# First mixture of an attention and two-mixture kernel: one pass over all 16 inner tiles, weights earlier, attention spread over more steps

## The chip, the cores and the metric

The kernel runs on one core of one Trainium2 chip. A core has five engines that run side by side, each through its own instructions in a fixed order: TensorE (PE, matrix products), VectorE (DVE), ScalarE (ACT), GpSimd (POOL) and SyncE (SP), which here issues nearly all DMAs. PE writes its products to PSUM, which DVE and ACT empty. The metric is the device time of one execution in microseconds (us); lower is better. The kernel before takes 1975.65 us (median of three runs, 1974.85 to 1976.97).

## The reference, cut to what matters

```python
# attention: batch 4, 8 heads, 576 positions, head size 64; float32
scores = q @ k.T / sqrt(64);  mask: a window of 32 positions for heads 0 to 3,
                              every 4th of 128 positions for heads 4 to 7
x = softmax(scores) @ v       # -> 2304 tokens x 512
# first mixture ("rational"): w_in 512 x 2048, w_out 2048 x 512, both float64
h = x @ w_in
P = a[0] + a[1]*h + a[2]*h*h + a[3]*h*h*h
Q = 1 + abs(b[0])*abs(h) + abs(b[1])*h*h
x2 = (P / (Q + 1e-6)) @ w_out
# second mixture: 8 experts, w1 512 x 1024 and w2 1024 x 512 each, float32
G = exp(x2 @ w_gate - max), then 8 rounds of normalising rows and columns
out = sum over e of G[:, e] * (relu(x2 @ w1[e]) @ w2[e])
```

The float64 weights reach the chip as pairs of 32-bit words; the kernel builds float32 values from them with integer operations.

## The kernel before, in words

The 2304 tokens are six blocks (n = 0 to 5) of 384; the 2048 inner columns are 16 tiles f of 128. One step of the first mixture is one (block, tile) pair: `rat_l1` (12 float16 matmuls, since each operand is split into a high and a low half) makes h in a PSUM bank, `rat_a`, `rat_q`, `rat_b` and `rat_c` form the rational function on DVE, ACT and POOL, and `rat_l2` (12 matmuls) adds the step's product with w_out to four PSUM banks `ob` that belong to the block. There are 96 steps. PE works on `rat_l1` of step g and `rat_l2` of step g - 5 (`LAG`).

`SEQ` (L620) is the order of the steps. The kernel before runs blocks 0 to 3 in two passes (L619): steps 0 to 31 take tiles 0 to 7 of blocks 0, 1, 2, 3, steps 32 to 63 take tiles 8 to 15 of the same blocks, and steps 64 to 95 all 16 tiles of blocks 4 and 5. At the end of a block's pass `x2_evac` (L710) empties the four banks: after the first pass by ACT copies (L717) into x2's place in SBUF, after the second by DVE additions to what lies there (L715).

The program falls into these stages. In the first, which I call the prelude, the attention of batch 0 runs, and the first quarters of w_in are loaded and converted. Then come the 96 steps with the attention of batches 1 to 3 strewn in by `ATT` (L1137): batch 1 over steps 0 to 7, batch 2 over 7 to 23, batch 3 over 40 to 62. A batch gives one and a half blocks. An attention batch is 52 pieces: 16 `prep` (transposes of q and k on PE, copies by ACT), 12 `qk`, 12 `tr` and 12 `av`. The second mixture follows, with its L1 products (L921) and L2 products (L1021 to L1023) on PE; its expert weights are prepared by DVE, ACT and POOL, those of expert 0 during steps 65 to 95 (`raw_absmax`, `raw_diff`, `raw_split`, L845 to L890).

Each step has four slots; `at(s, ...)` hangs work on slot s and `run_slot` runs it. So are hung: the conversion of w_in's quarters c = 1 to 3 (`wi_conv`, `wi_scale`, `wi_split`, from step `WI_S[c]` on, L1139), that of w_out's 16 tiles (`wo_split(f)` at step `WO[f]`, L1138, its load four slots ahead), the maximum over a finished block (`x2_absmax`, L721) and the mixing of two blocks for the second mixture (`mix_sub`, `mix_put`, L738, L742). Conversion of one 128x512 tile is `to_f32` (L489): one ACT copy (L492) and three DVE operations: a shift (L496), a shift with an or for the low bits (L497), an and with an or for the sign (L498). A w_in tile then has a pass for its maximum on ACT (L527) and a split by ACT and DVE (L229, L232); a w_out tile has a copy on ACT (L609) and a subtraction on POOL (L613).

Loads go out on SP's queue in order. `load` (L165) ties a load to the newest matmul that opens a step, so that loads are paced by PE. SBUF is laid out by hand (`HOME`): rooms R2 and R3 hold first q and k of attention pairs that are loaded ahead (`LOADS`, L1158) and later quarters 2 and 3 of w_in; room W3 holds a second pair of transposed q and k for batches 0 and 1 (`alt`, L336) and later the raw quarter 3.

The order in which each engine runs its instructions is not that of the program alone: a planner takes the instructions in program order as priority, attention pieces with a bonus, simulates when each is ready, and lets a later one pass an earlier one that is not ready. `pin` (L824) forbids this for one instruction: it must follow the one last noted in `behind`. Before, `pin` is used for weight preparation of the second mixture alone, and `behind` is empty during the 96 steps.

Of the kernel before, what the change touches and what calls it, by code (L numbers as in the profile page):

```python
# [22 lines left out]
SIGN = -(1 << 31)  # L23
# [5 lines left out]
def kernel(  # L29
# [20 lines left out]
    P = 128  # L50
# [180 lines left out]
    def split_lo(src, hi, lo, s):  # L231
        nc.vector.scalar_tensor_tensor(out=lo, in0=src, scalar=s, in1=hi, op0=ALU.mult, op1=ALU.subtract)  # L232
# [98 lines left out]
    def att_prep(b, pr, x):  # L331
# [4 lines left out]
        alt = b < 2 and pr % 2  # L336
# [152 lines left out]
    def to_f32(src, y, dst):  # L489
        w = src.rearrange("p (n two) -> p n two", two=2)  # L490
        lo, hi = w[:, :, 0], w[:, :, 1]
        nc.scalar.activation(y, hi.bitcast(F32), AF.Copy, scale=float(2.0**-112))  # L492
        d = y.bitcast(I32)

        def bits():
            nc.vector.tensor_scalar(out=d, in0=d, scalar1=3, scalar2=None, op0=ALU.logical_shift_left)  # L496
            nc.vector.scalar_tensor_tensor(out=d, in0=lo, scalar=29, in1=d, op0=ALU.logical_shift_right, op1=ALU.bitwise_or)  # L497
            nc.vector.scalar_tensor_tensor(out=dst.bitcast(I32), in0=hi, scalar=SIGN, in1=d, op0=ALU.bitwise_and, op1=ALU.bitwise_or)  # L498

# [44 lines left out]
    def wo_load(f):  # L544
        t = xhome(5 if f in (1, 3, 5) else 3)
# [26 lines left out]
    def wi_scale(c):  # L572
        return pow2_scale(wmx[:, 4 * c:4 * c + 4], 4, 14, s_wi[:, c:c + 1], i_wi[:, c:c + 1], lag=3 if c > 1 else 0, then=lambda: coefs(0, c, c + 1))
# [10 lines left out]
    def wg_prep():  # L584
        m = cols()
        nc.vector.tensor_reduce(out=m, in_=wgr.rearrange("p k e -> p (k e)"), axis=AX, op=ALU.max, apply_absolute_value=True)
        pow2_scale(m, 1, 4, s_wg, i_wg)
        split16(wgr, wg[:, :, 0:NE], wg[:, :, NE:], s_wg)()
# [28 lines left out]

    cur = {}
    PASSES = [(n, f0, f0 + 8) for f0 in (0, 8) for n in range(4)] + [(n, 0, NF1) for n in range(4, NB)]  # L619
    SEQ = [(n, f, f == f0, f == f1 - 1) for n, f0, f1 in PASSES for f in range(f0, f1)]  # L620
# [24 lines left out]
    def pair(st, x):  # L645
        if st // 2 % 2 == 0:
            return room(f"I{x}0", [P, 2, TB], F32)
        return room(f"I{x}1" + ("b" if 54 <= st < 78 else "a"), [P, 2, TB], F32)

    def rat_a(st):  # L650
# [6 lines left out]
        nc.vector.scalar_tensor_tensor(out=t, in0=t, scalar=a1, in1=hp, op0=ALU.add, op1=ALU.mult)  # L657
# [7 lines left out]
    def rat_b(st):  # L665
# [5 lines left out]
        nc.vector.scalar_tensor_tensor(out=g, in0=g, scalar=na0, in1=r, op0=ALU.add, op1=ALU.mult)  # L671
# [10 lines left out]
    def rat_l2(st, half):  # L682
# [11 lines left out]
        if half == 1:  # L694
            cur.pop(st)
            if last:
                x2_evac(n, f == NF1 - 1)
# [4 lines left out]
    x2p = {}  # L702
# [7 lines left out]
    def x2_evac(n, final):  # L710
        t = xhome(n).rearrange("p (k t) -> p k t", k=KD)
        part = x2p.pop(n, None)
        for dd in range(KD):
            if part is not None:
                nc.vector.tensor_tensor(out=t[:, dd, :], in0=ob[dd], in1=part[:, dd, :], op=ALU.add)  # L715
            else:
                nc.scalar.activation(t[:, dd, :], ob[dd], AF.Copy)  # L717
# [703 lines left out]
```

## Time and profile before

| | us |
|---|---|
| median of three runs (lowest, highest) | 1975.65 (1974.85, 1976.97) |
| the profiled execution's own time | 1978.19 |
| its span, first to last instruction | 1976.1 |
| busy: POOL | 491.1 |
| busy: PE's weight loads (PEld), beside the matmuls | 1418.3 |

The page of the profile gives busy times of each engine and, in 40 slices of about 49 us, the busy tenths and the TensorE clock that was granted, in tenths of full speed. A busy engine can be one that runs at half clock. The views that follow are windows (busy time of each engine between two moments), waits (who waited for whom), timelines (instructions in order) and groups of instructions by line. Line numbers are those of the kernel before. The windows below cut the span where PE starts the first L1 matmul of step 0 (68.93 us), of step 15 (207.31), of step 39 (318.62) and of step 60 (442.98), and where the last L2 matmul of step 95 ends (631.45). In a row of a window the busy times stand in the order PE, PEld, DVE, ACT, POOL; where a tile or a line is asked for, engines without such instructions are left out of it.

### The profile page before, as it was taken

How to read it: one execution, taken by the hardware profiler on the slowest of the kernel's cores; microseconds unless marked ns; L12 is line 12 of the kernel's file. 1: busy time of each engine (PE TensorE's matmuls, PEld its weight loads, DVE VectorE, ACT ScalarE, POOL GpSimd, SP SyncE). 2: the span in 40 equal slices, each digit the busy share in tenths (PEclk: the TensorE clock that was granted, in tenths of full speed). 3: DMA queues.
4: the chain of work that ended last, by engine and by line, in shares of the span. 5: the costliest groups of instructions: out<-in, count | busy, mean ns of one | idle time of the engine just before them, and what ended most of it. 6: DMA issues, size and time to landing. Idle time of an engine off the chain costs nothing. (4 is left out here: it accounts for less than half of the span.)

```text
span 1976.1 us, 36600 instructions
## 1 busy us (share of the span) xinstructions
PE 1886.4 (95%) x14202; PEld 1418.3 (72%) x14202; DVE 1567.5 (79%) x2564; ACT 1217.0 (62%) x2182; POOL 491.1 (25%) x489
## 2 busy tenths in 40 slices
PE   6688999998999999999999999999999999999998
PEld 5466777776767677767777777777777777777776
DVE  5797788799997998778787777877877787786754
ACT  5777777775776645646565664655555565555542
POOL 1232334321222113014212311411421141141111
PEclk7789999999999999999999999999999999999999
DMA  6643221124310451565356346345435625543323
GB/s 181 165 140 87 50 68 34 34 67 144 109 44 17 150 163 59 175 171 155 68 136 154 69 110 174 68 103 142 111 62 131 166 65 117 159 91 79 83 56 53
DMA packets 213133, 207.92 MB, mean 105 GB/s; under 512 B 78432, under 2 KB 160864, under 8 KB 212960
## 3 DMA queue, kind: packets, MB, share of 16 engines
q1 hardware_dynamic: 196096, 173.09, 29.1%
q0 software_dynamic: 16864, 32.51, 11.0%
q8 instruction: 111, 1.82, 0.4%
q14 instruction: 62, 0.51, 0.1%
HBM read 155.86 MB, written 49.68 MB: 104 GB/s over the span
## 5 line engine op out<-in xcount | busy, mean ns | idle before, releaser
L921 PEld LDWEIGHTS <-roomA 128*128 128x128 f16 x3276 | 319.7, 98 | 181.5 <-issue 14.6
L921 PE MATMUL l1a<-roomA 128*128 128x384 f16 x1872 | 357.0, 326 | 5.3 <-ACT roomV L970 4.2
L921 PE MATMUL l1b<-roomA 128*128 128x384 f16 x1404 | 273.6, 326 | 4.0 <-DVE roomA L972 1.9
L943 POOL TENSOR_TENSOR roomIG<-roomA 128x384 f32<-128x384 f32 x48 | 59.7, 1244 | 455.6 <-ACT roomA L977 354.6
L1021 PE MATMUL yps<-roomA 128*128 128x256 f16 x630 | 169.7, 273 | 2.2 <-DVE roomV L1047 1.5
L1022 PE MATMUL yps<-roomA 128*128 128x256 f16 x630 | 170.7, 273 | 0.8 <-DVE roomA L884 0.8
L1022 PE MATMUL yps<-roomA,roomV 128*128 128x256 f16 x630 | 170.5, 273 | 0.1
L677 POOL TENSOR_TENSOR roomIG<-roomA,roomIG 128x384 fp32r<-128x384 f32 x96 | 116.6, 1225 | 213.6 <-ACT roomIG L676 184.1
L1023 PE MATMUL yps<-roomA,roomV 128*128 128x256 f16 x630 | 169.6, 273 | 0.0
L1023 PE MATMUL yps<-roomA 128*128 128x256 f16 x630 | 168.9, 273 | 0.0
L1021 PE MATMUL yps<-roomA,roomV 128*128 128x256 f16 x630 | 168.8, 273 | 0.1
L692 PE MATMUL o1ps<-roomIG,roomV 128*128 128x384 f32 x384 | 136.2, 355 | 4.0 <-POOL roomIG L677 3.8
L870 POOL TENSOR_TENSOR roomA<-roomA 128x256 f32<-128x256 f32 x140 | 130.7, 953 | 35.2 <-DVE roomA L884 23.3
L631 PE MATMUL h1ps<-roomA 128*128 128x384 f16 x384 | 130.5, 340 | 8.8 <-ACT p L390 4.2
L884 DVE SCALAR_TENSOR_TENSOR roomA<-roomA,sm 128x768 f16<-128x768 f32 (+1 forms) x92 | 114.5, 1257 | 24.7 <-ACT roomA L881 23.9
L693 PE MATMUL o1ps<-roomIG,roomV 128*128 128x384 f32 x384 | 130.6, 340 | 0.0
L632 PE MATMUL h1ps<-roomA 128*128 128x384 f16 x384 | 130.1, 339 | 0.3 <-DVE roomA L232 0.3
L633 PE MATMUL h1ps<-roomA 128*128 128x384 f16 x384 | 129.8, 338 | 0.0
L943 POOL TENSOR_TENSOR roomIG<-roomV 128x384 f32<-128x384 f32 x48 | 50.1, 1044 | 299.5 <-ACT roomV L977 248.7
L691 PE MATMUL o1ps<-roomIG,roomV 128*128 128x384 f32 x384 | 107.5, 363 | 15.9 <-ACT roomIG L676 15.8
L1021 PEld LDWEIGHTS <-roomA 128*128 128x128 f16 x1008 | 98.7, 98 | 28.5 <-DVE roomA L1047 3.4
L881 ACT ACTIVATE roomA<-roomA,sm 128x768 f16<-128x768 f32 (+1 forms) x92 | 93.7, 1035 | 37.4 <-POOL roomA L870 17.8
(224 smaller groups left out, 4958.3 us busy)
## 6 DMA issues: line engine op xcount, KB each, us to landing
roomA<-xd SPq DMA_DIRECT2D x119, 384.0 KB
roomA<-in_moe_w_dram SPq DMA_DIRECT2D x256, 128.0 KB
roomA<-in_moe_w_dram SPq DMA_DIRECT2D x128, 256.0 KB
out_dram<-roomV POOLq DMA_DIRECT2D x31, 512.0 KB, 5.8
out_dram<-roomA POOLq DMA_DIRECT2D x31, 512.0 KB, 5.8
roomV<-in_moe_w_in_dram SPq DMA_DIRECT2D x16, 512.0 KB
roomA<-in_moe_w_out_dram SPq DMA_DIRECT2D x16, 512.0 KB
xd<-roomA SPq DMA_DIRECT2D x14, 384.0 KB
```

Source lines behind the costliest of these rows:

```text
L631: mm = nc.tensor.matmul(hp, whi, xb[:, 0, kk, :], start=kk == 0, stop=False)
L632: nc.tensor.matmul(hp, whi, xb[:, 1, kk, :], start=False, stop=False)
L633: nc.tensor.matmul(hp, wlo, xb[:, 0, kk, :], start=False, stop=kk == KD - 1)
L677: nc.gpsimd.tensor_tensor(out=gl, in0=g, in1=gh.bitcast(F32), op=ALU.subtract)
L692: nc.tensor.matmul(ob[dd], hi, d["gl"], start=False, stop=False)
L693: nc.tensor.matmul(ob[dd], lo, d["gh"], start=False, stop=last)
L870: pin("p" if pool else "v", eng.tensor_tensor(out=d[:, o, :], in0=a, in1=b, op=ALU.add if w == 0 and n == 0 else ALU.subtract))
L884: pin("v", nc.vector.scalar_tensor_tensor(out=l, in0=x, scalar=sc, in1=h, op0=ALU.mult, op1=ALU.subtract))
L921: mm = nc.tensor.matmul(ps, w[:, wx_, wh, kk * P:(kk + 1) * P], x[:, xh, kk, :], start=start and kk == 0 and wh == 0 and xh == 0, stop=sto ...
L1021: nc.tensor.matmul(o, hh[:, a - 1, c], w[:, m, 0, :], start=i == 0 and half == 0, stop=False)
L1022: nc.tensor.matmul(o, hh[:, a - 1, c], w[:, m, 1, :], start=False, stop=False)
L1023: nc.tensor.matmul(o, hl[:, a - 1, c], w[:, m, 0, :], start=False, stop=i == NP - 1 and (last or half == 1 or b == 3))
```

## The change

- The first mixture runs each block through all 16 tiles at once: steps 16n to 16n + 15 belong to block n. No partial sums remain; `x2_evac` is four ACT copies per block.
- So quarters 2 and 3 of w_in and tiles 8 to 15 of w_out are due at steps 8, 12 and, for w_out, 8 + 5 to 15 + 5. `WI_S` goes from (0, 8, 14) to (0, 4, 7.5), `WO` of tiles 8 to 15 from 20 to 34 to 11.75 to 16.75, the loads of the two quarters from 16 and 14 slots to 6 and 4 slots ahead of their step, and the lag in `wi_scale` from 3 slots to 1. w_out tiles are staged in two places in turn for all f.
- Attention: batch 1 over steps 0 to 14, batch 2 over 15 to 38, batch 3 over 39 to 62. R2, R3 and W3 are no longer free for batch 1, so its q and k are loaded one pair ahead only, and its transposed q and k have one place.
- `to_f32`: the ACT copy becomes a parametric relu with slope -2^32 for negative values, whose result keeps the sign in the right bit; the third DVE operation (L498) goes.
- The gate weights are loaded at step 20 and prepared at step 26 instead of in the prelude.
- x2 work (`x2_absmax`, `mix_sub`, the low half in `mix_put`) is tied by `pin` behind the newest of the rational function's DVE operations (L657 or L671, noted in `behind`). Since `behind` now holds an entry during the steps, the expert-0 preparations that used `pin` all along are tied too.

```diff
-SIGN = -(1 << 31)
...
     def split_lo(src, hi, lo, s):
-        nc.vector.scalar_tensor_tensor(out=lo, in0=src, scalar=s, in1=hi, op0=ALU.mult, op1=ALU.subtract)
+        return nc.vector.scalar_tensor_tensor(out=lo, in0=src, scalar=s, in1=hi, op0=ALU.mult, op1=ALU.subtract)
...
-        alt = b < 2 and pr % 2
+        alt = b < 1 and pr % 2
...
-        nc.scalar.activation(y, hi.bitcast(F32), AF.Copy, scale=float(2.0**-112))
+        nc.scalar.activation(y, hi.bitcast(F32), AF.Prelu, scale=float(2.0**-112), alpha=-float(2.0**32))
...
-            nc.vector.scalar_tensor_tensor(out=d, in0=lo, scalar=29, in1=d, op0=ALU.logical_shift_right, op1=ALU.bitwise_or)
-            nc.vector.scalar_tensor_tensor(out=dst.bitcast(I32), in0=hi, scalar=SIGN, in1=d, op0=ALU.bitwise_and, op1=ALU.bitwise_or)
+            nc.vector.scalar_tensor_tensor(out=dst.bitcast(I32), in0=lo, scalar=29, in1=d, op0=ALU.logical_shift_right, op1=ALU.bitwise_or)
...
-        t = xhome(5 if f in (1, 3, 5) else 3)
+        t = xhome(5 if f % 2 else 3)
...
-        return pow2_scale(wmx[:, 4 * c:4 * c + 4], 4, 14, s_wi[:, c:c + 1], i_wi[:, c:c + 1], lag=3 if c > 1 else 0, then=lambda: coefs(0, c, c + 1))
+        return pow2_scale(wmx[:, 4 * c:4 * c + 4], 4, 14, s_wi[:, c:c + 1], i_wi[:, c:c + 1], lag=1 if c > 1 else 0, then=lambda: coefs(0, c, c + 1))
...
-        pow2_scale(m, 1, 4, s_wg, i_wg)
-        split16(wgr, wg[:, :, 0:NE], wg[:, :, NE:], s_wg)()
+        return pow2_scale(m, 1, 4, s_wg, i_wg, lag=3, then=lambda: split16(wgr, wg[:, :, 0:NE], wg[:, :, NE:], s_wg)())
...
-    PASSES = [(n, f0, f0 + 8) for f0 in (0, 8) for n in range(4)] + [(n, 0, NF1) for n in range(4, NB)]
-    SEQ = [(n, f, f == f0, f == f1 - 1) for n, f0, f1 in PASSES for f in range(f0, f1)]
+    SEQ = [(n, f, f == 0, f == NF1 - 1) for n in range(NB) for f in range(NF1)]
...
-        return room(f"I{x}1" + ("b" if 54 <= st < 78 else "a"), [P, 2, TB], F32)
+        return room(f"I{x}1" + ("b" if 58 <= st < 78 else "a"), [P, 2, TB], F32)
...
-        nc.vector.scalar_tensor_tensor(out=t, in0=t, scalar=a1, in1=hp, op0=ALU.add, op1=ALU.mult)
+        behind["v"] = nc.vector.scalar_tensor_tensor(out=t, in0=t, scalar=a1, in1=hp, op0=ALU.add, op1=ALU.mult).ins.name
...
-        nc.vector.scalar_tensor_tensor(out=g, in0=g, scalar=na0, in1=r, op0=ALU.add, op1=ALU.mult)
+        behind["v"] = nc.vector.scalar_tensor_tensor(out=g, in0=g, scalar=na0, in1=r, op0=ALU.add, op1=ALU.mult).ins.name
...
-    def x2_evac(n, final):
+    def x2_evac(n):
         t = xhome(n).rearrange("p (k t) -> p k t", k=KD)
-        part = x2p.pop(n, None)
         for dd in range(KD):
-            if part is not None:
-                nc.vector.tensor_tensor(out=t[:, dd, :], in0=ob[dd], in1=part[:, dd, :], op=ALU.add)
-            else:
-                nc.scalar.activation(t[:, dd, :], ob[dd], AF.Copy)
-        if not final:
-            x2p[n] = t
+            nc.scalar.activation(t[:, dd, :], ob[dd], AF.Copy)
...
-        nc.vector.tensor_reduce(out=xmx[:, n:n + 1], in_=xhome(n), axis=AX, op=ALU.max, apply_absolute_value=True)
+        pin("v", nc.vector.tensor_reduce(out=xmx[:, n:n + 1], in_=xhome(n), axis=AX, op=ALU.max, apply_absolute_value=True))
...
-        nc.vector.tensor_tensor(out=mix_src(G, c), in0=mix_src(G, a), in1=mix_src(G, b), op=ALU.subtract)
+        pin("v", nc.vector.tensor_tensor(out=mix_src(G, c), in0=mix_src(G, a), in1=mix_src(G, b), op=ALU.subtract))
...
-            split_lo(src, t[:, 0, :], t[:, 1, :], s)
+            pin("v", split_lo(src, t[:, 0, :], t[:, 1, :], s))
...
-    ATT = ((1, 0, 7), (2, 7, 23), (3, 40, 62))
-    WO = [f + f // 7 if f < 8 else 20 + 2 * (f - 8) for f in range(NF1)]
-    WI_S = (None, 0, 8, 14)
+    ATT = ((1, 0, 14), (2, 15, 38), (3, 39, 62))
+    WO = [f if f < 8 else 11.75 + (f - 8) // 2 * 1.5 + 0.5 * (f % 2) for f in range(NF1)]
+    WI_S = (None, 0, 4, 7.5)
...
-    LOADS = {a: (c,) for a, c in zip(allp, allp[1:]) if a >= (1, 3)}
-    LOADS.update({(0, 2): ((1, 1, "R2"),), (0, 3): ((1, 0), (1, 3, "R3")), (1, 0): ((1, 2),), (1, 2): ((2, 0),)})
-    LOADS.pop((1, 3))
+    LOADS = {a: (c,) for a, c in zip(allp, allp[1:]) if a >= (0, 3)}
...
-            at(s + (14 if c > 1 else 11) + kk, wi_split, c, kk)
+            at(s + (12 if c > 1 else 11) + kk, wi_split, c, kk)
...
-        at(4 * WI_S[c] - (16 if c == 2 else 14), wi_load, c)
+        at(int(4 * WI_S[c]) - (6 if c == 2 else 4), wi_load, c)
+    at(4 * 20, lambda: load(wgr, w_gate.rearrange("(k p) e -> p k e", p=P)))
+    at(4 * 26 + 1, wg_prep)
...
-    nc.sync.dma_start(out=wgr, in_=w_gate.rearrange("(k p) e -> p k e", p=P))
...
-    extra[20] += [wg_prep]
```

## Rows read from the trace of the kernel before

**Rows 1.** Page: busy us with shares; PE busy and granted clock in tenths, 40 slices.

```profile
PE 1886.4 (95%) x14202; PEld 1418.3 (72%) x14202; DVE 1567.5 (79%) x2564; ACT 1217.0 (62%) x2182; POOL 491.1 (25%) x489
PE   6688999998999999999999999999999999999998
PEclk7789999999999999999999999999999999999999
```

**Rows 2.** Windows by stage: length, then each engine's busy us, clock, DMA share, GB/s.

```profile
0.00:68.93 68.93, 45.74 (x398) 35.53 (x399) 37.54 (x122) 38.95 (x146) 11.46 (x33) 0.69 0.73 196
68.93:207.31 138.38, 116.58 (x898) 84.22 (x899) 113.45 (x246) 105.26 (x303) 40.42 (x44) 0.88 0.39 112
207.31:318.62 111.31, 108.36 (x748) 81.57 (x747) 95.88 (x166) 86.43 (x194) 41.39 (x37) 0.98 0.21 57
318.62:442.98 124.36, 121.21 (x957) 95.28 (x955) 102.28 (x176) 95.27 (x231) 38.31 (x40) 1.00 0.17 45
442.98:631.45 188.47, 174.57 (x1074) 135.00 (x1071) 174.51 (x258) 129.15 (x214) 50.63 (x40) 0.96 0.26 81
631.45:1976.10 1344.65, 1319.90 (x10138) 986.74 (x10136) 1043.88 (x1600) 761.91 (x1099) 308.84 (x298) 1.00 0.45 113
```

**Rows 3.** Same windows, instructions on one tile: scps (twice), then qkps, scps, ptps, avps.

```profile
68.93:207.31 138.38, 19.77 (x247) 11.21 (x228) 7.96 (x18) 19.11 (x108) 0.88 0.39 112
318.62:442.98 124.36, 6.30 (x56) 5.88 (x56) 6.52 (x16) 1.00 0.17 45
318.62:442.98 124.36, 11.35 (x156) 6.29 (x144) 5.44 (x12) 12.89 (x72) 1.00 0.17 45
318.62:442.98 124.36, 5.56 (x33) 3.64 (x33) 5.32 (x11) 1.00 0.17 45
318.62:442.98 124.36, 6.60 (x108) 5.36 (x108) 4.68 (x15) 4.91 (x15) 1.00 0.17 45
```

**Rows 4.** Same windows, one line: L498 in two stages, then L497, L496, L492.

```profile
0.00:68.93 68.93, 5.72 (x8) 0.69 0.73 196
68.93:207.31 138.38, 12.69 (x16) 0.88 0.39 112
207.31:318.62 111.31, 7.12 (x8) 0.98 0.21 57
207.31:318.62 111.31, 4.03 (x8) 0.98 0.21 57
207.31:318.62 111.31, 5.43 (x8) 0.98 0.21 57
```

**Rows 5.** Timelines, prelude: start, us, engine, line, operation, [idle before and releaser]; SPq issues.

```profile
31.24 0.19 DVE L586 TENSOR_REDUCE sm<-wgr 128x1 f32<-128x32 f32 x1 [3.61 <-DMA wgr<-in_moe_w_gate_dram]
57.17 0.66 ACT L492 ACTIVATE roomV<-roomV 128x512 f32<-128x512 f32 x1 [5.95 <-DMA roomV<-in_moe_w_in_dram]
40.00 3.41 SPq L280 DMA_DIRECT2D roomA<-in_q_dram  x2
52.82 0.45 SPq L166 DMA_DIRECT2D roomV<-in_moe_w_in_dram  x1
```

**Rows 6.** Waits of PE, whole run: us in total, times, longest.

```profile
PE o1ps L691 <- ACT roomIG L676: 15.8, 8, 7.4
PE ptps L405 <- DVE roomA L232: 6.7, 2, 6.1
```

**Rows 7.** Timelines of DVE and ACT around 490 us.

```profile
482.77 1.94 DVE L715 TENSOR_TENSOR roomA<-o1ps,roomA 128x384 f32<-128x384 f32 x4
486.36 0.95 DVE L740 TENSOR_TENSOR roomA<-roomA 128x768 f32<-128x768 f32 x1
487.43 1.74 DVE L722 TENSOR_REDUCE sm<-roomA 128x1 f32<-128x1536 f32 x1
491.00 0.52 ACT L676 ACTIVATE roomIG<-roomA 128x384 fp32r<-128x384 f32 x1 [6.25 <-DVE roomA L671]
```

**Rows 8.** Groups by line, ACT: the only table load.

```profile
L239 ACT ACT_TABLE_LOAD x1 | 1.3, 1283 | 0.8 <-PEq L1405 0.8
```

More of the change, by code (lines that the diff above doesn't have):

```diff
@@ L615, in wo_split, with pin @@
         return s1
+    behind = {}
+    def pin(eng, i):
+        if eng in behind:
+            tc.add_manual_dep(i.ins, behind[eng], mybir.DependencyInfo(mybir.DependencyClass.Sync, mybir.DependencyReason.DATA), reason="behind work that others wait for")
     cur = {}
-    PASSES = [(n, f0, f0 + 8) for f0 in (0, 8) for n in range(4)] + [(n, 0, NF1) for n in range(4, NB)]
-    SEQ = [(n, f, f == f0, f == f1 - 1) for n, f0, f1 in PASSES for f in range(f0, f1)]
+    SEQ = [(n, f, f == 0, f == NF1 - 1) for n in range(NB) for f in range(NF1)]
     def rat_l1(st, half):
@@ L696, in rat_l2 @@
             if last:
-                x2_evac(n, f == NF1 - 1)
+                x2_evac(n)
     NG3 = NB // 2
     XQ = KD // 2 * TB
-    x2p = {}
     xmx = cols(NB)
@@ L821 @@
     ring = [0]
-    behind = {}
-    def pin(eng, i):
-        if eng in behind:
-            tc.add_manual_dep(i.ins, behind[eng], mybir.DependencyInfo(mybir.DependencyClass.Sync, mybir.DependencyReason.DATA), reason="after this group's h")
     def raw_load(e, k):
@@ L1201 @@
     for f in range(NF1):
-        at(4 * WO[f], wo_split, f)
+        at(int(4 * WO[f]), wo_split, f)
         if f >= 2:
-            at(4 * WO[f] - 4, wo_load, f)
+            at(int(4 * WO[f]) - 4, wo_load, f)
     def at_u(u, fn, *a):
@@ L1287 @@
     for c in range(1, 4):
-        s = 4 * WI_S[c]
+        s = int(4 * WI_S[c])
         for kk in range(KD):
             at(s + 1 + 2 * kk, wi_conv, c, kk)
-            at(s + (14 if c > 1 else 11) + kk, wi_split, c, kk)
+            at(s + (12 if c > 1 else 11) + kk, wi_split, c, kk)
         at(s + 10, wi_scale, c)
     for c in (2, 3):
-        at(4 * WI_S[c] - (16 if c == 2 else 14), wi_load, c)
+        at(int(4 * WI_S[c]) - (6 if c == 2 else 4), wi_load, c)
+    at(4 * 20, lambda: load(wgr, w_gate.rearrange("(k p) e -> p k e", p=P)))
+    at(4 * 26 + 1, wg_prep)
     for i in range(3):
@@ L1298 @@
     at(4 * (1 + 8), v_scale, 1)
-    at(4 * max(WI_S[3] + 4, 1 + 9), coefs, 1, 0, 4)
+    at(4 * 13, coefs, 1, 0, 4)
     att_load(0, 0)
```

## The prediction

> **What bounds the kernel now.** I read the page first. PE is busy for 95% of the span, but its slices show where it is not: 6 to 8 tenths in the first three, with a granted clock of 7 to 9 tenths, and 9 or more nearly everywhere after [rows 1]. So I cut the span by stage [rows 2]. From 631 us on PE is busy for 1319.9 of 1344.7 us at full clock: the second mixture is PE's, nothing in the change touches its work, and I carry it over at 0 (1.5 us either way for another order at its start). What can be won lies in the first 631 us.
>
> There the stages have different limits [rows 2]. Steps 15 to 38 and 39 to 59 are PE's: 108.4 of 111.3 and 121.2 of 124.4 us. The prelude is nobody's: PE 45.7, DVE 37.5, ACT 39.0 of 68.9 us, at a clock of 0.69. In steps 0 to 14 DVE is busy for 113.5 and ACT for 105.3 of 138.4 us, PE for 116.6, part of that slowly: a mean clock of 0.88 means that 24% of the stage was granted the half level, 33 us, in which up to 16.6 us of work were lost, so PE's work there is some 100 us at 2.4 GHz. In steps 60 to 95 DVE is the bound, 174.5 of 188.5 us. The waits of PE agree: the largest, 15.8 us, is that of the step's L2 matmuls for the ACT copy of the finished function, 7.4 us of it in one piece [rows 6], and the timelines show this piece: between 482.8 and 489 us DVE does four additions of partial sums (1.94 us), a subtraction of the mixing (0.95, three more follow) and a block's maximum (1.74) among the function's operations, and ACT idles for 6.25 us until DVE has finished the function [rows 7].
>
> **The change part by part: prelude.** Three things go. The gate weights' preparation: DVE, which takes its instructions in order, stands 3.61 us for their load [rows 5], and softmax work queues behind it. I count 0.5 us of that, since the next thing ACT and DVE meet is a wait for w_in anyway; the ends are 0 and 3.6. On SP's queue the loads of two pairs of batch 1 go; one of them is seen at 40.00 us, where issuing q alone takes 3.41 us, ahead of w_in's quarter 1, which is issued only at 52.82 [rows 5]. For that quarter ACT stands 5.95 us [rows 5], and PE waits 6.1 us meanwhile [rows 6]. Between the two stand loads of v that wait for PE, so I take 1.5 us of the 6, ends 0 and 6. Third, L498: 5.72 us for eight tiles [rows 4]; half of it lies where DVE has room, and 2 us count. Sum -4 us, between 0 and -8 (the three upper ends do not add up, since two of the waits follow one another on the same chain).
>
> **Steps 0 to 14.** Here the change moves work both ways, and I redo each engine's sum.
> - Out goes the part of batch 2 that ran here: 18 groups' maxima of scps are in this stage, and a batch has 12, so half of batch 2 [rows 3]. A whole batch is priced by the stage that holds batch 3 alone: PE 6.30 + 11.35 + 5.56 + 6.60 = 29.8 us, ACT 6.52 + 12.89 + 5.32 + 4.91 = 29.6, DVE 5.44 + 4.68 = 10.1 [rows 3]. Half is 15, 15 and 5 us.
> - Out goes L498 of the 16 tiles converted here: DVE -12.7 [rows 4].
> - In come six of the eight w_out tiles that were converted in steps 15 to 38 (tiles 8 to 13): a tile now costs DVE (7.12 + 4.03) / 8 = 1.4 us and ACT 5.43 / 8 = 0.68 for the conversion and, at the same price, once more for its copy [rows 4]: DVE +8.4, ACT +8. In come the splits of quarter 3, four tiles on each of the two, priced like L497 at 0.9 us on DVE and 0.7 on ACT: +3.5 and +3. The parametric relu is taken at the copy's price; the ends are 0 and the table loads below.
> - DVE: 113.5 - 12.7 - 5 + 8.4 + 3.5 = 107.7 us. ACT: 105.3 - 15 + 8 + 3 = 101. PE: 100 - 15 = 85.
>
> So PE is relieved most, and it is not the bound: DVE and ACT each lose only 4 to 6 us. The stage follows DVE's share of it. That was 113.5 / 138.4 = 0.82 with attention dense; it is 174.5 / 188.5 = 0.93 in steps 60 to 95 without attention [rows 2]. With 12 groups instead of 18 and conversions spread evenly I take 0.90, the nearer to the second: 107.7 / 0.90 = 120 us, that is -18. The ends are 0.82 (131 us, -7) and 0.95 (113 us, -25).
>
> **Steps 15 to 38.** The half batch lands on PE where PE is the bound: +15 us (15 to 17 with waits), 111.3 to 126. DVE's and ACT's relief here is worth nothing. L498 of eight tiles, the gate weights (one small matmul) and the first blocks' x2 copies lie beside PE. Steps 0 to 38 thus give -3 us in all, although single stages move by 15 to 18: the same PE work in another order, and only what stood idle can be won.
>
> **Steps 39 to 59.** PE has 3.2 us of idle [rows 2]. DVE loses twelve partial-sum additions here, off the path. -1 us (0 to -3).
>
> **Steps 60 to 95.** DVE, the bound, loses the four additions of block 3 (1.94 us) and the maximum of block 2, now finished eight steps earlier (1.74) [rows 7]: 174.5 - 3.7 = 170.8. The evacuation of block 3 goes to ACT, which is busy for 129 of 188 us [rows 2]. At DVE's share of 0.926 the stage takes 184.5 us: -4. The ties take no work away, they reorder: the subtractions and maxima no longer stand ahead of the function, which should break up the 7.4 us wait of PE, but DVE has the same queue to finish, so I count that wait only as DVE's work. The other end of the ties is that DVE stands idle for an ACT copy while tied work is ready; at a share of 0.90 the stage takes 190 (+1.5). If the ties let the expert's preparation slip into the second mixture, where DVE has 300 us to spare, the stage ends at about DVE's work and the last L2 matmuls, 171 + 5 = 176 us (-12).
>
> Edits at nothing: the single place for q and k of batch 1 (batch 3 works so within a stage that is 97% PE), the later switch of rooms at step 58, two staging places for w_out (a shorter wait on SP's queue). The shorter lag in `wi_scale` puts PE's small matmul one slot behind DVE's maximum; PE, with 35 us to spare in steps 0 to 14, pays for it. The moved DMAs: six w_out loads of 512 KB come into steps 0 to 14, 3 MB in 120 us or some 25 GB/s on top of 112, at a DMA share of 0.39 [rows 2], while half a batch's q, k and v leave; the gate weights' 16 KB load meets SP's queue at step 20, with the DMA share at 0.21. POOL's subtractions for the six tiles find it busy for 40 of 138 us [rows 2].
>
> **Sum.** -4 - 18 + 15 - 1 - 4 + 0 = -12 us on the profiled execution's 1978.2, so 1966. That execution lies 2.5 us over the median of 1975.65; on the median it is 1964 us. A change below 0.2% (4 us) cannot be told from none.
>
> **Rivals.**
> 1. *Late weights, slower.* Quarters 2 and 3 of w_in are loaded 6 and 4 slots ahead of their step instead of 16 and 14, into staging that the quarter before must have left, their last low halves are due in the very slot of step 8's matmuls, and six more w_out loads share SP's queue. ACT runs in order: a conversion whose load is late stops the softmax and the function behind it, as the 5.95 us at 57 us show [rows 5]. For: two quarters at 6 us and six w_out loads at 1 us make 18 us, and the first stage takes 138 us. Against: DVE and ACT, not PE, set the pace there, so slots are some 2 us long and a load has 8 us or more. Then -4 + 0 + 15 - 1 - 4 = +6: 1982. It decides from a first stage of 132 us on, where the sum is nought. Chance 0.18.
> 2. *No change.* DVE's share in steps 0 to 14 stays near 0.84 with the two in-order engines waiting for each other (128 us, -10), and the ties give back what steps 60 to 95 win (-1): -4 - 10 + 15 - 1 - 1 = -1: 1974. Chance 0.20.
> 3. *Far faster.* Both upper ends: 113 us in the first stage (-25), 176 us in the last (-12), -6 in the prelude: -6 - 25 + 15 - 1 - 12 = -29: 1947. For it speaks that PE's work of steps 0 to 38 is 100 + 106 us in 250, so 40 us lie open. Chance 0.17.
> 4. *The parametric relu needs another table.* The trace has one table load, 1.28 us [rows 8]. If the relu were in another set than the logarithm and exponential, each of 32 tiles would bring up to two loads, 64 x 1.28 = 82 us on ACT, two thirds of them in steps 0 to 14 beside 101 us of work: some 50 us more, 2015. Chance 0.03. The Trainium skill, "ScalarE: Activation LUTs", section "Table sets: the hidden batching unit", lists what makes this unlikely: cheap functions such as relu and copy are in every set. The same page, in "What ACT_TABLE_LOAD costs", gives about 2.66 us for a switch with its drain; by that figure the estimate would be twice as much. The trace, with Copy, Identity, Abs, Exp and Ln on one load, agrees as far as it goes; no row shows this relu.
>
> **Chances and range.** The forecast has 0.42 (its own range 1955 to 1971). Faster by over 0.2%: forecast and rival 3, 0.59; within 0.2%: rival 2, 0.20; slower: rivals 1 and 4, 0.21. The range runs from rival 3's 1947, rounded down, to rival 1's 1983.
>
> **What would show it.** Right: step 0 starts at 64 to 67 us; step 15 about 120 us later, with DVE's share near 0.9; step 39 126 us after that; one table load still; steps 60 to 95 near 184 us, without a wait of L2 on ACT of over 4 us. Wrong: over 132 us from step 0 to step 15, above all with ACT waiting for w_in or w_out; or a second mixture that is not 1345 us.

## The result, and the profile after

The changed kernel takes 1956.24 us (median of four runs, 1951.47 to 1956.99) beside 1975.25 us for the kernel before (four runs): a ratio of 0.9908, 95% interval 0.9891 to 0.9925, so 19 us faster. Its profiled execution took 1956.04 us, with a span of 1954.0.

The page after, the lines that answer to [rows 1] (busy us with shares; PE's busy tenths and granted clock in 40 slices):

```profile
PE 1876.0 (96%) x14202; PEld 1409.4 (72%) x14202; DVE 1545.2 (79%) x2516; ACT 1219.1 (62%) x2182; POOL 504.5 (26%) x489
...
PE   6689999999999999999999999999999999999998
...
PEclk6789999999999999999999999999999999999999
```

Only the first three slices and the last still show a PE under 9 tenths. The windows by stage, cut at the same events as [rows 2] (step 0, 15, 39, 60, the last L2 matmul of step 95); busy us of PE, PEld, DVE, ACT, POOL, then clock, DMA share, GB/s:

```profile
0.00:72.07 72.07, 45.00 (x396) 35.33 (x397) 37.09 (x113) 42.37 (x153) 11.39 (x33) 0.68 0.63 175
72.07:181.75 109.68, 92.94 (x701) 65.70 (x701) 98.99 (x215) 90.96 (x243) 40.16 (x39) 0.91 0.52 153
181.75:311.53 129.78, 128.20 (x975) 99.34 (x973) 101.64 (x180) 101.93 (x252) 44.63 (x44) 1.00 0.19 45
311.53:428.66 117.13, 115.86 (x905) 90.20 (x904) 85.55 (x151) 88.24 (x220) 38.66 (x36) 1.00 0.16 41
428.66:615.89 187.23, 176.73 (x1115) 135.18 (x1115) 176.74 (x262) 134.20 (x223) 57.41 (x40) 0.98 0.28 86
615.89:1954.00 1338.11, 1317.26 (x10117) 983.65 (x10115) 1045.17 (x1599) 761.37 (x1096) 312.29 (x298) 1.00 0.46 113
```

| stage | before, us | after, us | difference | forecast | PE idle plus lost to the half clock, before / after |
|---|---|---|---|---|---|
| prelude | 68.9 | 72.1 | +3.1 | -4 | 44.3 / 50.2 |
| steps 0 to 14 | 138.4 | 109.7 | -28.7 | -18 | 38.2 / 26.1 |
| steps 15 to 38 | 111.3 | 129.8 | +18.5 | +15 | 4.7 / 1.6 |
| steps 39 to 59 | 124.4 | 117.1 | -7.2 | -1 | 3.1 / 1.3 |
| steps 60 to 95 | 188.5 | 187.2 | -1.2 | -4 | 20.8 / 13.9 |
| second mixture | 1344.6 | 1338.1 | -6.5 | 0 | 26.7 / 25.7 |
| sum | 1976.1 | 1954.0 | -22.1 | -12 | 137.8 / 118.7 |

The last column is a stage's length less PE's busy time, plus half of the time for which the records show the granted clock at the lower level (1.2 GHz), which is the length times one less the mean clock of the row. In the fourteen profiles, the kernel before and every kernel below among them, the span less this sum lies between 1831 and 1839 us: PE's work is the same in all, and what a version wins or loses by more than these 8 us is idle time and half clock of PE. This is bookkeeping (the span less the sum is PE's busy time less half of the time at the lower clock): it tells where time went and not why, and differences of 4 to 6 us between versions are no larger than its spread. The single stages mislead, since work crosses their borders. Steps 15 to 38 hold 45 more L2 matmuls than before (288 instead of 243) and steps 39 to 59 24 fewer (264 instead of 288); steps 60 to 95 hold 72 of the second mixture's L1 matmuls instead of 51, 4.1 us of PE by the same windows.

PE's waits from step 0 to step 95 (total us, times, longest), to compare with [rows 6]:

```profile
PE o1ps L693 <- ACT roomIG L678: 7.2, 4, 3.1
PE mxps L179 <- DVE sm L206: 4.5, 1, 4.5
PE avps L428 <- ACT roomA L409: 3.1, 1, 3.1
```

The wait of L2 for the ACT copy of the finished function went from 15.8 to 7.2 us, and its longest piece from 7.4 to 3.1.

### The profile page after: what moved, and what is told of

Its sections match the earlier page's. It is cut to its first block, busy times and chain, and to the rows that moved or that the text cites. A ratio compares the mean times of both kernels' runs of the same rounds, so it can differ in the third digit from the quotient of the medians.

```text
span 1954.0 us, 36544 instructions
## 1 busy us (share of the span) xinstructions
PE 1876.0 (96%) x14202; PEld 1409.4 (72%) x14202; DVE 1545.2 (79%) x2516; ACT 1219.1 (62%) x2182; POOL 504.5 (26%) x489
## 3 DMA queue, kind: packets, MB, share of 16 engines
q0 software_dynamic: 16864, 32.51, 11.2%
## 5 line engine op out<-in xcount | busy, mean ns | idle before, releaser
L679 POOL TENSOR_TENSOR roomIG<-roomA,roomIG 128x384 fp32r<-128x384 f32 x96 | 126.5, 1328 | 222.8 <-ACT roomIG L678 206.6
L874 DVE SCALAR_TENSOR_TENSOR roomA<-roomA,sm 128x768 f16<-128x768 f32 (+1 forms) x92 | 113.5, 1247 | 19.8 <-ACT roomA L871 18.6
L1012 PEld LDWEIGHTS <-roomV 128*128 128x128 f16 x1008 | 98.5, 98 | 23.7 <-issue 0.6
```

The source lines that it names most:

```text
L679: nc.gpsimd.tensor_tensor(out=gl, in0=g, in1=gh.bitcast(F32), op=ALU.subtract)
L874: pin("v", nc.vector.scalar_tensor_tensor(out=l, in0=x, scalar=sc, in1=h, op0=ALU.mult, op1=ALU.subtract))
L1012: nc.tensor.matmul(o, hh[:, a - 1, c], w[:, m, 1, :], start=False, stop=False)
```

## The experiments

Each was timed in five rounds beside the kernel before, with a ratio to it. The changed kernel itself was run once more:

> The changed kernel once more, so that the others stand beside it on one chip: 0.991 of the kernel before. Both theories expect step 0 to start within 1 us of 72 us if the prelude's 3 us loss belongs to the change, and near 69 us if it was one execution's DMAs.

Measured: 1955.13 us, 0.9902 (0.9884 to 0.9919). Stages: 71.5, 109.3, 130.6, 117.1, 187.8 and 1336.4 us. So the stage lengths above repeat within 1.7 us in this pair. Step 0 is within 1 us of 72 again, but a third profile of the same order, further down, has 69.4: whether the prelude's loss belongs to the change stays open.

**Which edit brings it? The relu alone, in the old order.**

```
 (kernel before)
-  activation(y, hi, AF.Copy, scale=2**-112)
+  activation(y, hi, AF.Prelu, scale=2**-112, alpha=-2**32)
-  scalar_tensor_tensor(dst, hi, SIGN, d, bitwise_and, bitwise_or)
```

> The kernel before with the parametric relu and without the third DVE operation, nothing else. Theory A (steps 0 to 14 last as long as DVE's work there at its share of the stage): DVE loses 12.7 of 113.5 us in steps 0 to 14, at a share of 0.82 that is 15 us; the other stages are PE's and give at most 2: 1959 us. Theory B (the order does it: attention spread, one pass; the removed operation lay beside other work): within 3 us of the kernel before, 1973 to 1976.

Measured: 1980.64 us, 1.0032 (1.0018 to 1.0046): slower by 6 to 7 us in the medians, though VectorE lost 24 operations of some 0.77 us before step 15 [rows 4]. (The two profiled executions have nearly one span, 1976.7 and 1976.1 us.) Theory A falls, and theory B, within 3 us, did not have the loss. Steps 0 to 14 of this kernel (window as above):

```profile
68.17:203.84 135.67, 114.67 (x925) 83.17 (x926) 105.33 (x234) 107.01 (x311) 36.93 (x44) 0.89 0.40 117
```

VectorE has 105.3 us of work instead of 113.5, and the stage is only 2.7 us shorter; its share falls to 0.78. So in the old order the stage as a whole was not VectorE's. Steps 15 to 38 give it back: 118.0 us instead of 111.3.

**The new order without the relu.** The changed kernel with the copy and the third operation put back (the diff above, reversed).

> The changed kernel with the copy and the third DVE operation back. Theory A: some 20 of 32 tiles are converted in steps 0 to 14, 0.79 us each, 16 us of DVE at a share of 0.90, but some of it falls where DVE has room: 10 to 17 us over the changed kernel, 1966 to 1973. Theory B: 1956 to 1959.

Measured: 1973.8 us, 0.9993 (0.9982 to 1.0004): nothing is left of the gain. Steps 0 to 14:

```profile
71.79:194.13 122.34, 98.27 (x709) 69.09 (x709) 112.93 (x236) 95.10 (x246) 42.93 (x40) 0.88 0.45 132
```

VectorE has 13.9 us more work than in the changed kernel, and the stage is 12.7 us longer, at a share of 0.92. Theory B falls; theory A's 1966 to 1973 is just missed. In the new order VectorE's work does cost time when it grows.

**Everything but the new order.** The kernel before with the relu, the later gate weights and the ties.

```
 (changed kernel)
-  SEQ = [(n, f, f == 0, f == NF1 - 1) for n in range(NB) for f in range(NF1)]
+  PASSES, SEQ, x2_evac, ATT, WO, WI_S, LOADS as before
```

> The kernel before with the parametric relu, the later gate weights and the ties of x2 work, but its own two passes, attention steps and weight steps. Theory A: the relu's 15 us and 2 to 4 of the ties and the gate weights: 1955 to 1959, so the new order would be worth about nothing. Theory B: at most 5 us under the kernel before, 1970 or more.

Measured: 1970.59 us, 0.9981 (0.9970 to 0.9992). Steps 0 to 14:

```profile
66.86:200.95 134.09, 116.90 (x903) 84.82 (x902) 102.53 (x226) 103.45 (x300) 38.93 (x44) 0.87 0.40 117
```

VectorE's share is 0.76: again the old order does not follow it, as theory B had it. Relu, ties and gate weights in the old order give 3 to 4 us; the new order with ties and gate weights, but without the relu, gives nothing; all together give 19. The gain is not a sum of parts. (The old order with ties and gate weights but without the relu was not run, so what the relu costs or gives there beside the ties is not known.)

**How much is the thinner attention?** Batch 1 pressed into steps 0 to 7 again, all else as changed.

```
-  ATT = ((1, 0, 14), (2, 15, 38), (3, 39, 62))
+  ATT = ((1, 0, 7), (2, 15, 38), (3, 39, 62))
```

> The changed kernel with batch 1's attention over steps 0 to 7 again instead of 0 to 14, all else as changed. Theory A2 (in the new order steps 0 to 14 follow DVE's work at a share of 0.90 to 0.92, because the attention is thin; dense attention lowers the share to the 0.78 to 0.82 of the old order): DVE's 99 us at 0.82 is 121 us, 11 over the changed kernel, 0.996 of the kernel before. Theory C (only the summed work of the stage counts, however it is strewn): within 3 us of the changed kernel, 0.990 to 0.992.

Measured: 1970.74 us, 0.9980 (0.9967 to 0.9993): some 15 us of the 19 go. Theory C falls; theory A2 had 11 us. Steps 0 to 14 and 15 to 38:

```profile
69.75:185.36 115.61, 98.27 (x678) 70.56 (x677) 91.10 (x209) 86.46 (x233) 34.16 (x35) 0.80 0.47 141
185.36:326.79 141.43, 135.33 (x997) 106.21 (x996) 109.42 (x186) 106.74 (x261) 47.34 (x50) 0.98 0.18 45
```

In the first, VectorE is busy for 79% with less work than in the changed kernel, and PE's mean clock is 0.80, not 0.91: 45.3 us of the stage at the lower level instead of 18.7 to 23.8 in the three profiles of the changed kernel. Late loads are not the cause there: none of PE's waits in this stage is for a DMA. What was left behind makes the next stage 11.6 us longer.

**The ties.** The function no longer noted for the ties to follow.

```
-  behind["v"] = nc.vector.scalar_tensor_tensor(...).ins.name      (in rat_a and in rat_b)
+  nc.vector.scalar_tensor_tensor(...)
```

> The changed kernel without an entry in `behind` during the 96 steps, so that neither the x2 work nor expert 0's preparation is tied to the rational function. Theory A2: only steps 60 to 95 move, where DVE is the bound and its work stays the same: +3 us, up to +7 if the 7.4 us wait of the kernel before comes back with its slow clock; 0.991 to 0.994. Theory D (the ties make the gain in that stage and at the start of the second mixture): +8 us or more, 0.995.

Measured: 1960.1 us, 0.9927 (0.9908 to 0.9945). The interval overlaps that of the changed kernel, but the profile has the difference where the ties work, in steps 60 to 95: 191.1 us instead of 187.2 (187.8 in the repeat). The window, and PE's two largest waits in it:

```profile
427.30:618.38 191.08, 175.99 (x1074) 134.93 (x1071) 172.00 (x258) 130.55 (x221) 49.84 (x40) 0.97 0.26 80
```

```profile
PE o1ps L693 <- ACT roomIG L678: 7.5, 5, 3.9
PE h1ps L633 <- DVE roomA L659: 3.8, 1, 3.8
```

In the changed kernel these two are 3.0 and 0.4 us in that stage. VectorE has 4.7 us less work there without the ties and the stage is longer all the same, so the order of VectorE's queue matters and not its length alone. PE loses 20.2 us there, idle and half clock, against 13.9, 14.5 and 15.3 in the three profiles of the changed kernel. The medians are 4 to 5 us apart, as theory A2 had it. That the ties are worth all of it is not shown: the four other small edits below that lose (the gate weights, the additions and the two of w_in) lose as much, and the two of w_in, with the ties in place, have 190.3 and 190.0 us in this stage.

**The gate weights back in the prelude.**

```
-  at(4 * 20, load wgr);  at(4 * 26 + 1, wg_prep)
+  load wgr ahead of att_load(0, 3);  extra[20] += [wg_prep]
```

> The changed kernel with the gate weights loaded and prepared in the prelude again. Theory A2: 0.5 us of a 3.6 us wait counts, so 0.990 to 0.992. If the wait counts in full: 0.993.

Measured: 1961.46 us, 0.9933 (0.9912 to 0.9953). Prelude, steps 0 to 14 and steps 15 to 38:

```profile
0.00:65.50 65.50, 45.38 (x375) 34.95 (x376) 33.85 (x114) 39.38 (x144) 10.91 (x32) 0.64 0.68 191
65.50:187.15 121.65, 104.47 (x740) 73.25 (x741) 103.11 (x232) 98.85 (x259) 42.03 (x41) 0.84 0.46 141
187.15:311.38 124.23, 124.02 (x956) 96.60 (x955) 93.11 (x164) 97.94 (x244) 43.85 (x42) 1.00 0.18 46
```

The prelude is 4 to 7 us shorter than in the profiles of the changed kernel, not longer, steps 0 to 14 are 10 to 12 us longer and steps 15 to 38 some 6 shorter: step 39 starts at 311.4 us, as in the changed kernel (311.5). The prelude is shorter because less stands ahead of step 0: 24 of the 144 matmuls on avps, three of the four low halves of w_in and one w_out conversion have moved behind it. The profiled span is 1955.0, 1 us over it, while the medians differ by 5 to 6 us: the ratio fits the wait counted in full, the profile the 0.5 us. Whether this edit is worth anything stays open.

**The additions of the partial sums.** One VectorE operation over each bank again, after the copy, for blocks 0 to 3 (a maximum with what the copy left, which changes no value).

```
   nc.scalar.activation(t[:, dd, :], ob[dd], AF.Copy)
+  if n < 4: nc.vector.tensor_tensor(out=t[:, dd, :], in0=ob[dd], in1=t[:, dd, :], op=ALU.max)
```

> The changed kernel with four further DVE operations on PSUM after each of the first four blocks' copies (a maximum of the bank with its copy, the size and operands of the partial-sum additions that went). Theory A2: 16 x 0.5 us of DVE, three quarters of it where PE is the bound, the last four operations in steps 60 to 95: +2 us, 0.991 to 0.993. Theory E (the copies and additions hold up PE through the four banks): +1 us at each of four block ends, +4 or more, 0.993 or above.

Measured: 1961.96 us, 0.9937 (0.9916 to 0.9957). Steps 15 to 38 and 60 to 95:

```profile
179.52:314.68 135.16, 131.23 (x977) 102.89 (x976) 105.57 (x191) 101.66 (x252) 45.76 (x45) 0.97 0.18 44
431.14:621.86 190.72, 177.14 (x1112) 137.27 (x1109) 179.08 (x266) 135.93 (x224) 52.74 (x40) 0.96 0.27 85
```

At about 0.49 us each [rows 7], the eight operations of blocks 0 and 1 add 3.9 us to the first stage's VectorE work and the four of block 3 some 2 us to the other's; the stages grew by 5.4 and 3.5 us, of which the first is 3 us by step 39 (314.7 instead of 311.5 us), since step 15 starts 2 us earlier. In both, PE lost some full clock (0.97 and 0.96 beside 1.00 and 0.98). The first of them is PE's, and VectorE is busy for only 106 of its 135 us: cover in the sum of a stage did not hide the additions. (The second is no longer than in the two runs of w_in below, which add nothing there.) The interval allows both theories, and theory E's mechanism is not shown: in the first stage PE's one long wait, 2.2 us, is for an ACT operation of the softmax and not for the banks.

**Can the prelude be shortened?** In the changed kernel ScalarE waits twice for w_in (timeline of ACT: start, us, operation, idle before and releaser):

```profile
41.55 0.66 ACT L491 ACTIVATE roomV<-roomV 128x512 f32<-128x512 f32 x1 [5.52 <-DMA roomV<-in_moe_w_in_dram]
...
55.80 0.66 ACT L491 ACTIVATE roomV<-roomV 128x512 f32<-128x512 f32 x1 [4.64 <-DMA roomV<-in_moe_w_in_dram]
```

Two runs issue w_in earlier: ahead of v's last loads on the same queue, and on GpSimd's queue.

```
+  wi_load(0)                          # ahead of att_load_v(4) to att_load_v(7)
-  extra[12].append(lambda: wi_load(0))
```

> The changed kernel, but w_in's first quarter is issued on SP's queue ahead of the last four loads of v of the first batch, and not paced among the attention's pieces. In the changed kernel ScalarE waits 5.52 us for it at 41.55 us. Theory A, that the prelude is as long as its late w_in makes it: that wait goes, the second quarter's of 4.64 us stays, and the prelude falls from 72.1 to 67 to 69 us, the kernel to about 1952. Theory B, that the transfers themselves are the limit (a DMA share of 0.55 to 0.68 over the whole prelude): v comes later by what w_in comes earlier, the wait moves to another operand, and the prelude stays at 71 to 73 us or grows to 75.

Measured: 1959.86 us, 0.9924 (0.9911 to 0.9937). The prelude is 71.2 us. ACT's wait for w_in, and PE's first, up to 75 us:

```profile
ACT roomV L491 <- DMA roomV<-in_moe_w_in_dram: 9.3, 2, 7.8
```

```profile
PE qkps L346 <- DMA roomA<-in_q_dram: 9.9, 3, 5.2
```

The same wait of PE in the changed kernel, where the 4.3 us are the kernel's first wait and the other one is 1.95 us:

```profile
PE qkps L346 <- DMA roomA<-in_q_dram: 6.3, 2, 4.3
```

The first quarter, issued at 23.15 us instead of 35.90, costs ACT a wait of 1.46 us instead of 5.52. But ACT, sooner at the second, waits 7.83 us for it instead of 4.64, though that was issued 2.5 us earlier, and a q behind the moved loads (issued at 34.47 instead of 32.38) comes later to PE. That is theory B, with a loss of 4 to 5 us by the end that it did not give.

```
-  load(out=wst[c, kk], in_=src)
+  load(out=wst[c, kk], in_=src, q=nc.gpsimd if c < 2 else None)
```

> The changed kernel, but the loads of w_in's first two quarters are issued on GpSimd's DMA queue instead of SP's, where v's loads that wait for TensorE stand ahead of them. Theory A, that the queue's order makes w_in late: both waits of ScalarE for w_in (5.52 and 4.64 us) go or shrink below 2 us each, the prelude falls from 72.1 to 64 to 67 us and the kernel to 1949 to 1952. Theory B, that the engines of the transfers are the limit: the waits move to q, k or v, the prelude stays at 71 to 73 us and the time at 1955 to 1957.

Measured: 1960.34 us, 0.9923 (0.9910 to 0.9936). Its prelude and steps 0 to 14, and PE's first wait up to 75 us:

```profile
0.00:67.09 67.09, 42.60 (x396) 33.67 (x397) 36.11 (x113) 43.08 (x153) 16.47 (x41) 0.73 0.69 188
67.09:179.68 112.59, 94.02 (x702) 66.03 (x702) 100.15 (x215) 91.50 (x244) 40.05 (x39) 0.90 0.50 149
```

```profile
PE qkps L346 <- DMA roomA<-in_q_dram: 11.1, 2, 6.7
```

ScalarE's waits for w_in are gone, as theory A had it, and the prelude is 2 to 5 us shorter than in the three profiles of the changed kernel; PE waits longer for q, as theory B had it. Step 15 starts 1 to 2 us earlier, and by the end the kernel is 4 to 5 us slower. Neither theory had that. The stages 15 to 38 and 60 to 95 and the second mixture are each 2 to 3 us longer than in the first profile of the changed kernel; why is not shown.

**Does less VectorE work shorten steps 0 to 14?** First by the slot alone:

```
-  at(4 * 13, coefs, 1, 0, 4)
+  at(4 * 24, coefs, 1, 0, 4)
```

> The changed kernel with one piece of VectorE work taken out of steps 0 to 14: the twelve small operations that form the function's coefficients for the second half of the tokens (first used at step 48) run at step 24 instead of step 13. In the trace of the changed kernel they take some 3.8 us of VectorE (twelve of the fifteen that take 4.73 us from 150 to 164 us). Theory A, that steps 0 to 14 follow VectorE's work at a share of 0.90 in the changed order: the stage falls from 109.7 by 3.8 / 0.90 = 4.2 us to 105.5, steps 15 to 38 stay near 130 since TensorE bounds them, and the kernel takes 1951 to 1953 us beside 1956. Theory B, that late in the stage ScalarE or TensorE sets the pace: the stage stays within 1 us of 109.7 and the time within 1 us of the changed kernel's.

Measured: 1954.72 us, 0.9901 (0.9886 to 0.9916). It tells nothing of the theories: the planner drew the twelve operations back to where they were, and on every engine the instructions stand in the changed kernel's order. It is a third profile of the changed kernel, and a measure of how far one order varies:

```profile
0.00:69.37 69.37, 42.78 (x396) 33.23 (x397) 36.83 (x113) 42.15 (x153) 11.46 (x33) 0.70 0.64 182
69.37:180.72 111.35, 95.04 (x701) 67.05 (x701) 99.69 (x215) 91.33 (x244) 39.22 (x39) 0.89 0.50 150
```

Step 0 starts between 69.4 and 72.1 us in the three, step 15 between 180.7 and 181.8. So the work was taken out for good:

```
-  at(4 * 13, coefs, 1, 0, 4)
+  at(4 * 24, coefs, 1, 0, 4)          # and each operation of it tied behind["v"]
-  in_=t[:, j * NV // 2:(j + 1) * NV // 2]
+  in_=t[:, j * NV // 2:j * NV // 2 + (32 if hf else NV // 2)]
```

> The changed kernel with VectorE relieved in steps 0 to 14. The coefficients for the second half of the tokens (twelve operations, some 3.8 us) are tied behind the function of step 24, since the planner drew them back to step 13 when only their slot was moved. And the maximum over v's second half looks at 32 of the 384 columns of each of its six pieces: that leaves part of the scan out, and makes six operations of 0.937 us into six of about 0.15 to 0.17 (the price of a maximum over 4 to 6 columns). Together VectorE loses 3.8 + 4.6 = 8.4 us before step 15. Step 0 moved between 69.4 and 72.1 us in three runs of one and the same order, so I compare step 15's start, which was 180.7 to 181.8 us. Theory A, that VectorE's work sets this stage at a share of 0.90: step 15 starts 8.4 / 0.90 = 9.3 us earlier, at 171 to 173 us, and the kernel takes 1946 to 1948 us. Theory B, that the share is what this order happens to give and ScalarE (91 us of work in 110), its waits and TensorE at half clock come next: step 15 starts at 177 to 181 us, VectorE's share falls to 0.83 to 0.87, and the time is 1951 to 1955.

Measured: 1956.21 us, 0.9905 (0.9890 to 0.9920), no change. Steps 0 to 14 and 15 to 38:

```profile
68.48:178.96 110.48, 93.12 (x709) 67.79 (x709) 92.67 (x209) 91.21 (x246) 39.92 (x41) 0.92 0.50 153
178.96:311.47 132.51, 128.08 (x970) 99.02 (x969) 102.01 (x189) 99.66 (x250) 43.35 (x43) 1.00 0.18 44
```

VectorE has 92.7 us of work instead of 99.0, its share is 0.84, and step 15 starts at 179.0 us where theory A asked for 171 to 173 (for 6.3 us in place of 8.4 it would be some 174). Theory A falls for the stage as a whole, and theory B gave the place and the share, with a time 1 us too low. What was won by step 15 is gone at step 39 (311.47 us, as in the changed kernel). In seven of the eleven profiles in the new order step 39 starts between 311.2 and 312.0 us, though step 15 starts between 179.0 and 187.2 in them; why is not shown.

The share of a stage is an average, and finer windows say more. Steps 3 to 8 of the changed kernel, of the one without the relu and of this one, then steps 12 to 14 of the changed kernel:

```profile
88.04:141.83 53.79, 43.50 (x307) 31.18 (x306) 52.30 (x103) 46.41 (x120) 22.49 (x19) 0.91 0.55 168
88.56:153.37 64.81, 47.63 (x308) 33.49 (x307) 63.76 (x119) 48.18 (x122) 24.37 (x21) 0.84 0.45 137
85.75:140.27 54.52, 43.26 (x307) 32.00 (x306) 51.33 (x104) 45.87 (x120) 20.67 (x19) 0.91 0.51 157
166.00:181.75 15.75, 15.75 (x117) 11.20 (x117) 13.72 (x32) 13.68 (x34) 6.75 (x7) 0.89 0.52 142
```

In steps 3 to 8 VectorE is nearly full (0.97), and without the relu 11.5 us more work cost 11.0 us there. In the last run only 1.0 of the 6.3 us came off these steps; the rest came off steps where VectorE was less full (0.69 in steps 0 to 2, 0.91 in steps 9 to 11 and 0.87 in steps 12 to 14, where TensorE is busy throughout). So the run hardly tests a relief where VectorE is the limit.

## Why the prediction was right, and where it was not

The direction held, and of the mechanism the part that the experiments bear out: attention spread thin and less conversion work together relieve steps 0 to 14. The total was under-estimated by a third or more (12 us forecast, 19 in the medians, 22 in the profiles), and that the sum came as near is luck in part: the prelude, steps 15 to 38 and steps 60 to 95 were 13 us worse than forecast, the other stages 23 us better. Up to step 39 it was as forecast (7 us); from there on 15 us came instead of 5. One of its own signs of being wrong, a second mixture that is not 1345 us, came true (1338.1). By its own steps:

- *Prelude, -4: not found (+3.1; +2.6 and +0.4 in the two other profiles of the same order, each against the one profile before).* The loads of batch 1 did leave the queue, and w_out's first is issued earlier, at 58.21 us instead of 63.66. But w_in's second quarter is issued at 51.66 instead of 52.82, 1.2 us earlier, and the wait for it is 4.64 instead of 5.95. The step that failed is that relieved engines would let step 0 start: the planner filled the room with work of the weights, and where less of it stood ahead, in the run with the early gate weights, step 0 started at 65.5 us. SPq and PE after, and SPq before:

```profile
51.66 1.86 SPq L165 DMA_DIRECT2D roomV<-in_moe_w_in_dram  x4
...
58.21 2.27 SPq L165 DMA_DIRECT2D roomA<-in_moe_w_out_dram  x2
```

```profile
70.33 1.81 PE L428 MATMUL avps<-roomA 96*64 96x64 f32 x24 [3.88 <-ACT roomA L409]
```

```profile
63.66 1.19 SPq L166 DMA_DIRECT2D roomA<-in_moe_w_out_dram  x2
```

  PE's last attention matmuls wait 3.88 us for an ACT copy that stands behind w_in's high halves and two w_out conversions, and ACT's work in the prelude rose from 39.0 to 42.4 us.

- *Steps 0 to 14, -18: right in kind, too small (-28.7).* The forecast was 107.7 us of VectorE's work at a share of 0.90; measured were 99.0 at 0.90. The share was right, the work was not. I had let six more w_out tiles into this stage, 22 in all, although `WO` itself puts tile 13 at step 15.25. The windows of the last conversion operation, after, for the prelude, steps 0 to 14 and steps 15 to 38:

```profile
0.00:72.07 72.07, 7.26 (x10) 0.68 0.63 175
72.07:181.75 109.68, 14.54 (x18) 0.91 0.52 153
181.75:311.53 129.78, 3.97 (x4) 1.00 0.19 45
```

  There are 18: ten went into the prelude instead of eight, and four still run after step 15. These 18 took 24.7 us of VectorE where the sum has 28.0 for 22, which is 3.3 of the missing 8.7 us. The splits, which the sum had growing by 3.5 us with quarter 3 and shrinking by 2.3 with the half batch, fell by 2.5 (18.5 to 16.0): quarter 1's four went into the prelude, whose splits grew from 5.63 to 8.04 us. So part of the prelude's loss is this stage's gain. The rest are smaller terms that partly cancel: small softmax operations that the price of a batch left out, fewer operations of the function, more of the coefficients. Step 15 starts 25.6 us earlier than before, against a forecast of 22.

  The reason behind the share was borne out only on one side. "The stage follows DVE's share of it" is true of the new order when VectorE gets more to do (12.7 us of time for 13.9 of work, in the run without the relu). It did not show when VectorE got less (the last run, which took little off the steps where VectorE is full), and it is not true of the old order (shares of 0.82, 0.78 and 0.76 at three different loads). The Trainium skill, "Perfetto Trace Analysis", section "Identifying the Most-Contended Engine", says to optimise first the engine with the highest occupancy. Taken over the whole stage that pointed at VectorE, with 0.90, and a relief of 6.3 us did not shorten the stage. By the finer windows it held for steps 3 to 8, where VectorE is nearly full, and not for steps 12 to 14, where PE is busy throughout. Over the whole stage ScalarE, with 91 us of work (101 in the forecast), PE, with 93 (and 19 us of the stage at the lower clock), and VectorE are none of them full; what a relief in steps 3 to 8 alone would give was not tried.

- *Steps 15 to 38, +15: right (+18.5).* The half batch came, 15 us of PE as priced (though the stage that gave the price holds only 108 of a batch's 144 matmuls on avps), and with it 45 L2 matmuls from the neighbouring stages. Step 39 starts 7.1 us earlier than before; the forecast was 7.

- *Steps 39 to 59, -1: too small (-7.2).* PE's idle time and half clock give 1.8 us of it; the rest is work that crossed the stage's borders, above all the 24 L2 matmuls that now run before step 39. From step 15 to 59 together it is +11.2 against +14.

- *Steps 60 to 95, -4, and the second mixture, 0: the split was wrong (-1.2 and -6.5).* 21 more L1 matmuls of the second mixture run before step 95 ends, 4.1 us. With these put back the first is -5.3 and the second -2.4. VectorE's work did not fall to 170.8 us, it rose to 176.7: the additions and one maximum went, but two more subtractions of the mixing and some of the function's operations fell into the stage. So it was not a shorter queue, as I had it, that helped. PE's loss in this stage fell by 6.9 us, and the run without the ties, with a loss of 20.2, points to the order in the queue. In the old order the ties changed little (20.7 before, 20.2 in the run with everything but the order). The 7.4 us wait is no measure of the ties: without them the longest is 3.9 us, and with the relu alone in the old order 3.2. VectorE was never the only bound here: before, PE was busy for as long (174.57 and 174.51 us) [rows 2].

- *The relu at the price of the copy, one table load: right.* The groups by line after, on ACT, beside [rows 8]; the copy's mean before was 676 and 677 ns:

```profile
L491 ACT ACTIVATE roomA<-roomA 128x512 f32<-128x512 f32 x16 | 10.9, 686 | 3.2 <-DMA roomA<-in_moe_w_out_dram 3.0 <-issue 0.2
L491 ACT ACTIVATE roomV<-roomV 128x512 f32<-128x512 f32 x16 | 10.8, 673 | 12.7 <-DMA roomV<-in_moe_w_in_dram 12.6
L238 ACT ACT_TABLE_LOAD x1 | 1.3, 1283 | 0.8 <-PEq L1393 0.8
```

  Rival 4 did not come. The rule of the Trainium skill that spoke against it ("ScalarE: Activation LUTs", section "Table sets: the hidden batching unit": relu and copy are in every set) agrees with this trace: the parametric relu, the relu and the copy live with the exponential and logarithm on one load.

- *Rival 1, late weights,* needed a first stage of over 132 us. It was 109.7; in it ACT waits 2.5 us for w_in and 2.4 for w_out. *Rival 2* wanted 128 us there. *Rival 3* had 113 us for it, which was beaten, but its 176 us in steps 60 to 95 and its -6 in the prelude did not come. (The range's upper end, 1983, is 1982 by rival 1's own sum.)

## What to carry to other kernels

Where one engine's work is the same in all versions, add up what that engine loses, idle time and half clock, over the whole run: that sum followed the span within 4 us in fourteen profiles, while the length of single stages moved by up to 29 us, in part because work crossed their borders. A share of 0.9 is an average: here it was VectorE nearly full in some steps and TensorE full in others, so more work cost time and less work elsewhere gave none. Cut the stage finer, and remove or add work where the engine is full, before building on a share. And edits of this kind do not add: the cheaper conversion cost some 6 us in the old order (without the ties) and won some 18 in the new (with them), so an edit that loses by itself is to be tried again with the others.

## What the runs showed of the hardware that I had not expected

- One and the same order of instructions on all engines gave a step 0 at 69.4, 71.5 and 72.1 us, and a step 15 at 180.7 to 181.8: the prelude varies by 2.7 us between executions, and the next stage takes most of that up.
- The same batch of attention, pressed into half the steps, cost more by clock than by idle time: idle of PE in steps 0 to 14 went from 16.7 to 17.3 us, time at 1.2 GHz from 18.7 (22.2 and 23.8 in the two repeats) to 45.3.
- Moving eight loads (two quarters of w_in) to GpSimd's queue took ScalarE's 10.2 us of waits for them away; PE then stood up to 6.7 us for loads of q, which had stayed on their queue (2.0 before the move, but for the first wait of the kernel).
